# The attention stage's product order: a written table of single steps in place of a fixed rhythm

## The chip, the cores and the metric

The kernel runs on one core of one Trainium2 chip. The metric is the device time of one execution in microseconds (us). In the rows, PE is TensorE's matmuls, PEld its weight loads, DVE is VectorE, ACT is ScalarE, POOL is GpSimd and SP is SyncE. A change of under 0.3% is about what a measurement of this kernel can't tell from none.

## The reference, cut to what matters

Three layers follow each other: retention over blocks of 64 positions, a two-layer MLP with a norm ahead of it, and a causal attention of four heads (`E = 4`, called experts there) with a gate that weights each head's output per position. Only the last is touched:

```
logits = x @ w_gate;  w = softmax over the two best heads
for e in range(E):
    q, k, v = x @ wq[e], x @ wk[e], x @ wv[e]
    scores = causal(scale * (q @ k.T));  a = softmax(scores)
    ye = a @ v @ wo[e]
    out += (weight of head e, where it is among the two best) * ye
```

The shapes are 2 batches, 768 positions, model width 512, 4 heads of 64.

## The kernel before, in words

The retention and the MLP fill the first 327 us or so. Then comes the attention. TensorE's instructions stand in the order in which the code calls them (PE is scheduled by hand throughout). In the attention stage the other engines' order is made by the scheduler from the program.

The 1536 positions are four blocks of 384 (`NBLK`). For each block `qkv_steps` gives eight steps: three stretches of products for the values and the gate's logits (`value`, tile `pv`, line L786), the gate's arithmetic on DVE (`gate`, L797 to L817, with no product on PE), and four projections for queries and keys (`proj`, tile `pj`, L764). Each projection's accumulator is emptied by ACT and DVE (`qs` L771 and L772, `kh` L775, `kl` L776), and POOL copies the keys across the halves (L778). The steps of block 0 stand ahead of the loop. The 24 of blocks 1 to 3 are handed out between the attention's own steps.

The attention itself works on 12 row tiles of 128 positions, in the order `ROWS`, with 4 heads each: 48 items, numbered 0 to 47. Row tile `t` has `t + 1` tiles of 128 keys. An item goes through these steps:

- `att_s` (s): scores on PE (tile `s`, L844, one product with `kh` and one with `kl` for each 512 columns), then mask and maximum on DVE and the exponential on ACT. They lie in one of two large accumulators (`big`).
- `att_c` (c): DVE forms one over the sum and POOL scales the probabilities (`att`, L871).
- `att_t` (t): PE transposes them in 128 x 128 tiles (tile `t`, L881), and ACT copies them out to a tile `aT` (L882).
- `att_av` (v): once for each pair of heads, the products of the values with `aT` (tile `av`, L893). Two heads stand in the two 64-row halves of the output. The trace counts two records for one of these products. After a row's second pair, ACT (L899) and DVE (L900) take the result out as `avs`.
- `att_o` (o): the output product of the row from `avs` (tile `o`, L914), copied out by DVE and stored.

The accumulators of `pv`, `pj`, `t`, `av` and `o` are four buffers (`mid`) that go round.

The order was a rhythm: in turn `k` the loop calls s of item `k`, then as many of the 24 steps as a count up to `FILL = 36` asks for, c of item `k - 1`, t of item `k - 5` (`LAG`), v of the pair that ends with item `k - 7`, and o of the row that ends with item `k - 10`. A row's two stretches of v are therefore two turns apart; the last row alone has them together.

Of the kernel before, what the change touches and what calls it, by code (L numbers as in the profile page):

```python
# [8 lines left out]
F32 = mybir.dt.float32  # L9
# [8 lines left out]
P = 128  # L18
B, H, S, D = 2, 8, 768, 64
# [7 lines left out]
NBLK = B * S // TB  # L27
NTB = TB // P
# [19 lines left out]
IN_WA = ((2, 2), (3, 1), (3, 2), (0, 3), (4, 1), (5, 1))  # L48

IN_DQ = ((6, 1), (7, 1), (4, 2), (5, 2))  # L50
FILL = 36
AV_AT, O_AT = 2, 5

ROWS = ((0, 0), (0, 1), (0, 2), (0, 3), (0, 4), (1, 2), (0, 5), (1, 5), (1, 1), (1, 4), (1, 3), (1, 0))
LAG = 5
NG = FT // GF
E = 4
HD = 64
# [4 lines left out]

F64_MIN = 2.0 ** -15
F64_MAX = 122879.9921875


@with_exitstack
def model(ctx, tc, qkT, kv, lam, g_ln, w12, wat, out):
# [23 lines left out]
    def ps_mid(name):  # L93
        return psum.tile([P, 512], F32, tag="mid", bufs=4, name=name)
# [64 lines left out]
    for n, gb in enumerate(groups):  # L159
        if n == 0:  # L160
            continue
        more = []
        if n >= NBLK - 1 and n + 1 < len(groups):
            more = [("g1", *groups[n + 1], f) for f in range(GF)]
        if gb == (1, 0):
            more = [("g1", 1, 2, f) for f in range(2, GF)]
        elif gb == (1, 1):
            more = []
# [18 lines left out]
    while rest:  # L187
        for p in rest:
            ft, i = p
# [28 lines left out]
    def prep_parts(ft, i):  # L218
# [11 lines left out]
        def clamp():  # L230
            mag = t["mag"]
            nc.vector.tensor_scalar(mag, mag, F64_MAX, F64_MIN, ALU.min, ALU.max)
            nc.vector.tensor_scalar(mag.bitcast(I32), mag.bitcast(I32), 3, 0x3FFFFFFF,
# [364 lines left out]
    def mlp_step():  # L598
        n = len(steps) - len(todo)
        due = [k for k in plan if k <= n]  # L600
        if due:
            plan.pop(min(due))
        decode(1 if due else 0)
        f, args, leave = step()
        leave()
        return f, args
# [111 lines left out]
    while todo:  # L718
        f, args = mlp_step()
# [15 lines left out]
    at = ctx.enter_context(tc.tile_pool(name="at", bufs=2, side="right", reuse_waits="tile"))  # L735
# [123 lines left out]
    def att_c(b, t, e):  # L859
        row = ROW[b, t]  # L860
        n = (t + 1) * P
        pair = n <= 512
        if pair and e % 2 == 0:
            return
        for f in ((e - 1, e) if pair else (e,)):
            c = at.tile([P, 1], F32, tag="c", name=f"c{b}{t}{f}", bufs=4)
            nc.vector.tensor_scalar(c, row["ssum"][:, f:f + 1], SUM_EPS, None, ALU.add)
            nc.vector.reciprocal(c, c)  # L868
            a = row["a"][f]
            gw = GW[2 * b + t // NTB][:, t % NTB, f:f + 1]  # L870
            nc.gpsimd.tensor_scalar(a[:, :n], a[:, :n], c, gw, ALU.mult, ALU.mult)  # L871

    def att_t(b, t, e):
        row = ROW[b, t]
        a = row["a"].pop(e)
        aT = row["aT"][e] = at.tile([P, S], F32, tag="aT", name=f"aT{b}{t}{e}", bufs=6)
        for j0 in range(0, t + 1, 4):
            j1 = min(j0 + 4, t + 1)
            pt = ps_mid(f"t{b}{t}{e}{j0}")
            for j in range(j0, j1):  # L880
                nc.tensor.transpose(pt[:, (j - j0) * P:(j - j0 + 1) * P], a[:, j * P:(j + 1) * P], ident)  # L881
            nc.scalar.copy(aT[:, j0 * P:j1 * P], pt[:, :(j1 - j0) * P])  # L882

    def att_av(b, t, pr):
        row = ROW[b, t]
        v = VV[b]
        if pr == 0:
            row["pav"] = ps_one(f"av{b}{t}")
        pav = row["pav"]
        for j in range(t + 1):  # L890
            for e2 in range(2):
                e = 2 * pr + e2
                nc.tensor.matmul(pav[e2 * HD:(e2 + 1) * HD, pr * P:(pr + 1) * P], v[:, j, e * HD:(e + 1) * HD],  # L893
                                 row["aT"][e][:, j * P:(j + 1) * P], start=(j == 0), stop=(j == t),
                                 skip_group_check=True)
        if pr == 1:
            av = row["av"] = at.tile([P, 2, 2, P], F32R, tag="av", name=f"avs{b}{t}")
            pv = pav[:, :2 * P].rearrange("p (a c) -> p a c", a=2)
            nc.scalar.copy(av[:, 0], pv)  # L899
            nc.vector.tensor_tensor(av[:, 1], pv, av[:, 0].bitcast(F32), ALU.subtract)  # L900

    def att_o(b, t):
        av = ROW.pop((b, t))["av"]
        wo = WA[3].rearrange("p a (m c) -> p a m c", m=2)
        o = at.tile([P, DM], F32, tag="o", name=f"os{b}{t}")

        halves = 2 if (b, t) == ROWS[-1] else 1
        for j in range(halves):
            cs = ts(j * DM // halves, (j + 1) * DM // halves)
            po = ps_one(f"o{b}{t}{j}")  # L910
            i = 0
            for (wi, xi) in PASSES:
                for pr in range(2):
                    nc.tensor.matmul(po[:, cs], av[:, xi, pr, :], wo[:, wi, pr, cs], start=(i == 0), stop=(i == 5))  # L914
                    i += 1
            if j == 0:
                nc.vector.tensor_copy(o[:, cs], po[:, cs])
            else:
                nc.scalar.copy(o[:, cs], po[:, cs])
            (nc.sync, nc.scalar)[j].dma_start(out[b, t * P:(t + 1) * P, cs], o[:, cs])  # L920
# [2 lines left out]
        step()  # L923

    more = [step for blk in range(1, NBLK) for step in qkv_steps(blk)]
    per_blk = len(more) // (NBLK - 1)
    items = [(b, t, e) for b, t in ROWS for e in range(E)]
    done = 0
    for k in range(len(items) + LAG + O_AT + 1):
        if k < len(items):  # L930
            b, t, e = items[k]
            while done < per_blk * (2 * b + t // NTB):
                more[done]()
                done += 1
            att_s(b, t, e)
            while done < min(len(more), len(more) * (k + 1) // FILL):
                more[done]()
                done += 1
        i = k - 1
        if 0 <= i < len(items):  # L940
            att_c(*items[i])
        i = k - LAG
        if 0 <= i < len(items):
            att_t(*items[i])
        i = k - LAG - AV_AT
        if 0 <= i < len(items) and items[i][2] % 2 == 1 and i < len(items) - 1:
            b, t, e = items[i]
            att_av(b, t, e // 2)
            if i == len(items) - 3:
                att_av(b, t, 1)  # L950
        i = k - LAG - O_AT
        if 0 <= i < len(items) and items[i][2] == 3:
            att_o(*items[i][:2])


# [52 lines left out]
```

## Time and profile before

| | |
|---|---|
| median of 3 runs | 466.61 us (465.85 to 467.31) |
| the profiled execution | 466.95 us |
| its span, first to last instruction | 465.2 us |
| granted TensorE clock, mean | 1.000 |
| PE busy | 453.3 us, 97% |
| DVE, ACT, POOL busy | 334.6, 208.5, 86.6 us |

The profiled execution's time is 1.75 us longer than its span. PE's recorded end of a matmul is modelled and runs past the start of the next one, so this text takes what a product costs from start to start: the start of a row in the timeline to the start of the next row.

### The profile page before, as it was taken

The numbers are of one execution on the slowest core, as the hardware profiler recorded it, in microseconds if no ns is written. First come the engines' busy times: TensorE is split into PE (matmuls) and PEld (weight loads), VectorE is DVE, ScalarE is ACT, GpSimd is POOL, SyncE is SP. The second block draws the span as 40 slices with busy tenths as digits, with TensorE's granted clock in tenths as the row PEclk, the third lists the DMA queues.
The fourth block names the chain that finished last, engine by engine and source line by source line (L and its number), as shares of the span: only waits on it lengthen the run. The fifth ranks groups of instructions, "written<-read, shape, count | busy, mean of one in ns | idle before, by whom it ended". The sixth has DMA issues, their size and how long they took to land.

```text
span 465.2 us, 9098 instructions
## 1 busy us (share of the span) xinstructions
PE 453.3 (97%) x3562; PEld 421.0 (91%) x3563; DVE 334.6 (72%) x698; ACT 208.5 (45%) x476; POOL 86.6 (19%) x132
## 2 busy tenths in 40 slices
PE   8789999999999999999999999999999999999997
PEld 4666779999999999999999999999998898998885
DVE  5887988869778778537789745646788686586663
ACT  3568675445433213113225311311466666557673
POOL 6745500000000000000000000000055443344340
PEclk9999999999999999999999999999999999999999
DMA  7997115634421222101224412220000000001011
GB/s 281 409 359 269 48 61 190 197 90 135 138 91 50 87 92 77 60 0 47 90 92 129 155 35 51 56 65 1 0 1 0 25 25 24 23 2 38 33 45 70
DMA packets 15226, 42.33 MB, mean 91 GB/s; under 512 B 2240, under 2 KB 5072, under 8 KB 15184
## 3 DMA queue, kind: packets, MB, share of 16 engines
q1 hardware_dynamic: 14896, 41.62, 26.3%
q8 instruction: 28, 0.46, 0.4%
q10 hardware_dynamic: 288, 0.13, 0.1%
q14 instruction: 14, 0.11, 0.1%
HBM read 35.43 MB, written 6.32 MB: 90 GB/s over the span
## 4 chain that ended last, share of the span: by engine, by line
PE 73%; DVE 8%; ACT 3%; issue 1%; POOL 0%; ACTq 0%; DVEq 0%
PE y L548 27%; PE h L514 23%; PE s L844 5%; PE av L893 4%; PE t L881 4%; PE o L914 4%; PE pj L764 3%; PE pv L786 3%; DVE qs L772 1%; PE yf L570 1%; DVE kl L776 1%; DVE w L255 1%; ACT att L856 1%; DVE xn L454 0%; ACT xn L451 0%
## 5 line engine op out<-in xcount | busy, mean ns | idle before, releaser
L514 PE MATMUL h<-xn,w 128*128 128x384 f32 x768 | 139.8, 336 | 0.0
L514 PEld LDWEIGHTS h<-xn,w 128*128 128x128 f32 x768 | 133.4, 188 | 2.8 <-issue 0.8
L548 PE MATMUL y<-hs,w 128*128 128x384 f32 x552 | 99.7, 334 | 0.0
L548 PEld LDWEIGHTS y<-hs,w 128*128 128x128 f32 x552 | 96.1, 188 | 0.0
L533 ACT ACTIVATE hs<-h 128x384 fp32r<-128x384 f32 x50 | 24.5, 490 | 108.6 <-PE h L514 99.0
L778 POOL TENSOR_SCALAR kh<-kh 64x384 fp32r<-64x384 f32 x16 | 8.1, 507 | 293.1 <-ACT kh L775 291.3
L534 DVE SCALAR_TENSOR_TENSOR hs<-h,hs 128x384 fp32r<-128x384 f32 x50 | 27.7, 554 | 34.6 <-ACT hs L533 34.5
L871 POOL TENSOR_SCALAR att<-att,c,gw 128x128 f32<-128x128 f32 (+5 forms) x48 | 35.6, 747 | 51.9 <-DVE c L868 16.0
L556 DVE TENSOR_TENSOR xT<-xT,y 128x768 f32<-128x768 f32 x24 | 22.8, 951 | 28.3 <-PE y L548 28.3
L243 ACT CAST w<-top 128x512 fp32r<-128x512 f32 x32 | 19.9, 621 | 42.3 <-DVE top L237 42.3
L764 PE MATMUL pj<-x,wa 128*128 128x384 f32 x192 | 35.0, 337 | 0.0
L764 PEld LDWEIGHTS pj<-x,wa 128*128 128x128 f32 x192 | 33.3, 188 | 0.0
L882 ACT COPY aT<-t 128x512 f32<-128x512 f32 (+3 forms) x64 | 26.5, 441 | 11.2 <-PE t L881 11.0
L881 PE MATMUL t<-ident,att 128*128 128x128 f32 x168 | 26.2, 275 | 0.5 <-DVE qs L772 0.5
L252 DVE TENSOR_TENSOR top<-top,w 128x512 f32<-128x512 f32 x32 | 24.0, 750 | 0.0
L893 PE MATMUL av<-aT,v 128*64 128x128 f32 x336 | 23.7, 280 | 0.0
L844 PE MATMUL s<-kh,qs 128*128 128x512 f32 (+3 forms) x64 | 23.3, 365 | 0.0
L248 DVE SCALAR_TENSOR_TENSOR mag<-raw,mag 128x512 f32<-128x512 uint32 x31 | 22.6, 729 | 0.7
L237 DVE SCALAR_TENSOR_TENSOR top<-raw,mag 128x512 int32<-128x512 int32 x31 | 22.2, 718 | 0.5
L228 ACT ACTIVATE mag<-raw 128x512 f32<-128x512 f32 x31 | 20.5, 669 | 4.2 <-DVE w L255 2.1
L255 DVE TENSOR_TENSOR w<-top,mag 128x512 fp32r<-128x512 f32 x32 | 21.9, 684 | 0.4
L893 PEld LDWEIGHTS av<-aT,v 128*64 128x64 f32 x336 | 18.0, 136 | 4.2 <-issue 3.5
(137 smaller groups left out, 702.1 us busy)
## 6 DMA issues: line engine op xcount, KB each, us to landing
raw<-in_w SPq DMA_DIRECT2D x31, 512.0 KB, 3.7
qk<-in_qkT SPq DMA_DIRECT2D x9, 512.0 KB, 6.5
kvn<-in_kv SPq DMA_DIRECT2D x9, 512.0 KB, 6.7
xd<-xT SPq DMA_DIRECT2D x4, 768.0 KB, 4.4
xr<-xd SPq DMA_DIRECT2D x8, 384.0 KB, 3.2
out<-os SPq DMA_DIRECT2D x11, 256.0 KB, 2.0
early<-in_qkT SPq DMA_DIRECT2D x3, 512.0 KB, 8.6
early<-in_kv SPq DMA_DIRECT2D x3, 512.0 KB, 4.6
```

What stands on the lines that cost most here:

```text
L252: nc.vector.tensor_tensor(t["top"], t["top"], t["w"][:, 0].bitcast(F32), ALU.subtract)
L255: nc.vector.tensor_tensor(t["w"][:, 1], t["top"], t["mag"], ALU.add)
L514: nc.tensor.matmul(ph[:, :TB], w[:, wi, k, :], xn[:, xi, k, :], start=(i == 0), stop=(i == 11))
L533: LAST.append((nc.scalar.activation(h[:, 0], ph[:, :TB], AF.Relu), nc.vector.scalar_tensor_tensor(h[:, 1], ph[:, :TB], 0.0, h[:, 0].bitcas ...
L534: nc.vector.scalar_tensor_tensor(h[:, 1], ph[:, :TB], 0.0, h[:, 0].bitcast(F32), ALU.max, ALU.subtract)))
L548: nc.tensor.matmul(y[:, j, :TB], w[:, wi, e * P:(e + 1) * P], h[:, xi], start=(f == 0 and i == 0), stop=(f == GF - 1 and i == 2))
L764: nc.tensor.matmul(ps[:, :TB], w[:, wi, k, :], x2[:, xi, k, :], start=(i == 0), stop=(i == 11))
L844: nc.tensor.matmul(ps[:, c0:c1], q, kk[:, e, c0:c1], start=(i == 0), stop=(i == 1))
L871: nc.gpsimd.tensor_scalar(a[:, :n], a[:, :n], c, gw, ALU.mult, ALU.mult)
L881: nc.tensor.transpose(pt[:, (j - j0) * P:(j - j0 + 1) * P], a[:, j * P:(j + 1) * P], ident)
L882: nc.scalar.copy(aT[:, j0 * P:j1 * P], pt[:, :(j1 - j0) * P])
L893: nc.tensor.matmul(pav[e2 * HD:(e2 + 1) * HD, pr * P:(pr + 1) * P], v[:, j, e * HD:(e + 1) * HD], row["aT"][e][:, j * P:(j + 1) * P], star ...
```

## The change

The loop of turns goes, and with it `FILL`, `AV_AT`, `O_AT` and `LAG`. A table `ORDER` names every step in order: a letter for the step and the item's number, and `f` for the next of the 24 steps of the blocks. A row's two v stand next to each other, in 11 of the 12 rows (items 32 to 35 keep them apart). The tile `aT` has eight buffers (`AT_BUFS`) instead of six.

```diff
-FILL = 36
-AV_AT, O_AT = 2, 5
-LAG = 5
+ORDER = """
+    s0 s1 f f s2 s3 c0 s4 c1 c2 s5 c3 f s6 c4 s7 t0 t1 f c5 f t2 c6 f t3 s8 c7 s9 t4 c8 s10 v1 v3 t5 c9 c10 f t6
...
+AT_BUFS = 8
...
-        aT = row["aT"][e] = at.tile([P, S], F32, tag="aT", name=f"aT{b}{t}{e}", bufs=6)
+        aT = row["aT"][e] = at.tile([P, S], F32, tag="aT", name=f"aT{b}{t}{e}", bufs=AT_BUFS)
...
-    for k in range(len(items) + LAG + O_AT + 1):
-        if k < len(items):
-            b, t, e = items[k]
-            while done < per_blk * (2 * b + t // NTB):
-                more[done]()
-                done += 1
+    more = iter(more)
+    for op in ORDER.split():
+        if op == "f":
+            next(more)()
+            continue
+        b, t, e = items[int(op[1:])]
+        if op[0] == "s":
             att_s(b, t, e)
-            while done < min(len(more), len(more) * (k + 1) // FILL):
-                more[done]()
-                done += 1
-        i = k - 1
-        if 0 <= i < len(items):
-            att_c(*items[i])
-        i = k - LAG
-        if 0 <= i < len(items):
-            att_t(*items[i])
-        i = k - LAG - AV_AT
-        if 0 <= i < len(items) and items[i][2] % 2 == 1 and i < len(items) - 1:
...
+        elif op[0] == "v":
             att_av(b, t, e // 2)
...
```

PE has the same instructions before and after. Three places show how they moved. The line numbers of the change are 10 higher. A row's x12 counts the same instruction 12 times over.

The first place is PE at the start of the attention, where row tile (0, 0) (items 0 to 3, tile `av_3755` before) meets its values. This is before, from the transposes of item 3 to the second pair:

```order
L881 MATMUL t_3752<-ident,att_3601 128x128
L893 MATMUL av_3755<-aT_3668,v_3397 64x128
L893 MATMUL av_3755<-aT_3684,v_3397 64x128
L844 MATMUL s_3719<-kh_3395,qs_3398 128x384
L844 MATMUL s_3719<-kl_3396,qs_3398 128x384
L881 MATMUL t_3766<-ident,att_3610 128x128 x2
L844 MATMUL s_3771<-kh_3395,qs_3398 128x384
L844 MATMUL s_3771<-kl_3396,qs_3398 128x384
L764 MATMUL pj_3774<-x_1_3158,wa_2873 128x384 x12
L881 MATMUL t_3800<-ident,att_3636 128x128 x2
L893 MATMUL av_3755<-aT_3712,v_3397 64x128
L893 MATMUL av_3755<-aT_3751,v_3397 64x128
```

This is the change, where the tile is `av_3771`, from the transposes of item 4 on:

```order
L891 MATMUL t_3763<-ident,att_3602 128x128 x2
L854 MATMUL s_3768<-kh_3395,qs_3398 128x384
L854 MATMUL s_3768<-kl_3396,qs_3398 128x384
L903 MATMUL av_3771<-aT_3654,v_3397 64x128
L903 MATMUL av_3771<-aT_3658,v_3397 64x128
L903 MATMUL av_3771<-aT_3712,v_3397 64x128
L903 MATMUL av_3771<-aT_3737,v_3397 64x128
L891 MATMUL t_3780<-ident,att_3614 128x128 x2
L774 MATMUL pj_3792<-x_1_3158,wa_2873 128x384 x12
L891 MATMUL t_3810<-ident,att_3643 128x128 x2
```

The two stretches of `av` were 8 rows apart, each behind transposes. They are one now, and it stands behind scores.

The second place is PE at the output product of row tile (1, 1) (items 32 to 35; its values are `av_4921` before and `av_4948` now). This is before: the end of the next row's first stretch (`av_5023`), and then the output product `o_5049`, whose own values had ended 22 rows ahead of it:

```order
L893 MATMUL av_5023<-aT_4933,v_3545 64x128
L893 MATMUL av_5023<-aT_4965,v_3545 64x128
L844 MATMUL s_5002<-kh_3543,qs_3546 128x128
L844 MATMUL s_5002<-kl_3544,qs_3546 128x128
L881 MATMUL t_5042<-ident,att_4908 128x128 x4
L914 MATMUL o_5049<-wa_3004,avs_4979 128x512 x6
```

This is the change, from the same row's last values to its output product:

```order
L903 MATMUL av_4948<-aT_4901,v_3545 64x128
L903 MATMUL av_4948<-aT_4912,v_3545 64x128
L903 MATMUL av_4948<-aT_4901,v_3545 64x128
L903 MATMUL av_4948<-aT_4912,v_3545 64x128
L891 MATMUL t_5000<-ident,att_4892 128x128 x4
L891 MATMUL t_5006<-ident,att_4892 128x128
L854 MATMUL s_5012<-kh_3543,qs_3546 128x128
L854 MATMUL s_5012<-kl_3544,qs_3546 128x128
L924 MATMUL o_5024<-wa_3004,avs_4996 128x512 x6
```

Between a row's last values and its output product there are now four groups: the transposes of one item and one small pair of scores products.

The third place is PE at block 3's projections. This is before: the last `pv` stretch and the four projections follow each other, and then come the scores of item 28:

```order
L881 MATMUL t_4427<-ident,att_4234 128x128 x3
L786 MATMUL pv_4432<-wa_2957,x_3_3376 128x260 x12
L764 MATMUL pj_4471<-x_3_3376,wa_2873 128x384 x12
L764 MATMUL pj_4488<-x_3_3376,wa_2910 128x384 x12
L764 MATMUL pj_4509<-x_3_3376,wa_2873 128x384 x12
L764 MATMUL pj_4526<-x_3_3376,wa_2910 128x384 x12
L844 MATMUL s_4550<-kh_3543,qs_3547 128x512
L844 MATMUL s_4550<-kl_3544,qs_3547 128x512
L844 MATMUL s_4550<-kh_3543,qs_3547 128x256
L844 MATMUL s_4550<-kl_3544,qs_3547 128x256
L881 MATMUL t_4563<-ident,att_4267 128x128 x3
```

This is the change, from the block's second `pv` stretch to its second projection:

```order
L796 MATMUL pv_4365<-wa_2957,x_3_3376 128x260 x12
L796 MATMUL pv_4379<-wa_2957,x_3_3376 128x260 x12
L891 MATMUL t_4394<-ident,att_4208 128x128 x3
L854 MATMUL s_4408<-kh_3395,qs_3542 128x512
L854 MATMUL s_4408<-kl_3396,qs_3542 128x512
L854 MATMUL s_4408<-kh_3395,qs_3542 128x256
L854 MATMUL s_4408<-kl_3396,qs_3542 128x256
L891 MATMUL t_4417<-ident,att_4225 128x128 x3
L774 MATMUL pj_4451<-x_3_3376,wa_2873 128x384 x12
L891 MATMUL t_4469<-ident,att_4259 128x128 x3
L774 MATMUL pj_4474<-x_3_3376,wa_2910 128x384 x12
L903 MATMUL av_4495<-aT_4215,v_3397 64x128
```

The third `pv` stretch, two items' transposes and a scores step now stand ahead of the first projection, and a row's whole stretch of values (20 such products) stands between the second and the third.

## Rows read from the trace of the kernel before

**Rows 1.** The page: span, busy time of PE, granted clock in 40 equal slices

```profile
span 465.2 us, 9098 instructions
PE 453.3 (97%) x3562; PEld 421.0 (91%) x3563; DVE 334.6 (72%) x698; ACT 208.5 (45%) x476; POOL 86.6 (19%) x132
...
PEclk9999999999999999999999999999999999999999
```

**Rows 2.** Waits of weight loads, 320 to 466 us: total us, times, longest us

```profile
PEld av L893 <- issue: 3.5, 20, 0.3
```

**Rows 3.** PE timeline, 371 to 376 us: start us, us, instruction, count

```profile
371.67 0.62 PE L881 MATMUL t<-ident,att 128*128 128x128 f32 x4
372.05 1.65 PE L914 MATMUL o<-wa,avs 128*128 128x512 f32 x6
373.53 0.40 PE L844 MATMUL s<-kh,qs 128*128 128x512 f32 x1
...
374.17 0.62 PE L881 MATMUL t<-ident,att 128*128 128x128 f32 x4
374.72 0.88 PE L893 MATMUL av<-aT,v 128*64 128x128 f32 x12
375.53 0.50 PE L844 MATMUL s<-kh,qs 128*128 128x512 f32 x1
```

**Rows 4.** PE timeline: scores behind transposes, and transposes behind values

```profile
367.24 0.49 PE L881 MATMUL t<-ident,att 128*128 128x128 f32 x3
367.49 0.48 PE L844 MATMUL s<-kh,qs 128*128 128x512 f32 x1
...
456.71 1.09 PE L893 MATMUL av<-aT,v 128*64 128x128 f32 x16
457.74 0.44 PE L881 MATMUL t<-ident,att 128*128 128x128 f32 x2
458.11 0.94 PE L893 MATMUL av<-aT,v 128*64 128x128 f32 x8
```

**Rows 5.** The page's weight loads of `pj`, and three `pj` stretches in PE's timeline

```profile
L764 PEld LDWEIGHTS pj<-x,wa 128*128 128x128 f32 x192 | 33.3, 188 | 0.0
...
378.79 6.52 PE L764 MATMUL pj<-x,wa 128*128 128x384 f32 x36
385.14 0.34 PE L844 MATMUL s<-kh,qs 128*128 128x384 f32 x1
```

**Rows 6.** PE timeline where it stood still; in brackets idle us and who ended it

```profile
341.19 0.22 PE L844 MATMUL s<-kh,qs 128*128 128x128 f32 x1
341.55 0.33 PE L844 MATMUL s<-kl,qs 128*128 128x128 f32 x1
...
351.64 0.33 PE L844 MATMUL s<-kl,qs 128*128 128x384 f32 x1
352.49 0.41 PE L881 MATMUL t<-ident,att 128*128 128x128 f32 x2 [0.51 <-DVE qs L772]
...
417.63 1.68 PE L914 MATMUL o<-wa,avs 128*128 128x512 f32 x6 [0.24 <-DVE kl L776]
```

**Rows 7.** DVE timeline: two subtractions that those waits ended on

```profile
351.78 0.56 DVE L772 SCALAR_TENSOR_TENSOR qs<-pj,qs 64x384 fp32r<-64x384 f32 x1
...
417.02 0.56 DVE L776 TENSOR_TENSOR kl<-pj,kh 64x384 fp32r<-64x384 f32 x1
```

**Rows 8.** From a row's last values to `avs`: slowest case, then quickest (PE, DVE)

```profile
420.60 0.88 PE L893 MATMUL av<-aT,v 128*64 128x128 f32 x12
...
423.62 0.41 DVE L900 TENSOR_TENSOR avs<-av,avs 128x256 fp32r<-128x256 f32 x1
...
458.26 0.42 DVE L900 TENSOR_TENSOR avs<-av,avs 128x256 fp32r<-128x256 f32 x1 [0.86 <-ACT avs L899]
```

More of the change, by code (lines that the diff above doesn't have):

```diff
@@ L65 @@
 F64_MAX = 122879.9921875
+ORDER = """
+    s0 s1 f f s2 s3 c0 s4 c1 c2 s5 c3 f s6 c4 s7 t0 t1 f c5 f t2 c6 f t3 s8 c7 s9 t4 c8 s10 v1 v3 t5 c9 c10 f t6
+    f s11 s12 t7 s13 f t8 c11 o3 f t9 s14 t10 c12 s15 v5 c13 v7 s16 c14 f t11 s17 c15 c16 t12 c17 s18 o7 v9 v11
+    f s19 t13 f t14 f f o11 c18 f t15 s20 c19 s21 t16 s22 c20 t17 v13 v15 s23 t18 s24 f o15 s25 c21 t19 c22 c23
+    s26 t20 c24 f f t21 c25 c26 s27 t22 f c27 f t23 f v17 v19 f f s28 s29 t24 c28 o19 c29 t25 s30 v21 v23 t26
+    s31 s32 t27 o23 t28 s33 c30 t29 s34 c31 c32 s35 v25 v27 c33 c34 c35 t30 s36 c36 o27 t31 s37 c37 t32 s38 v29
+    c38 v31 t33 s39 t34 s40 t35 s41 t36 o31 c39 c40 v33 c41 s42 t37 s43 t38 v35 c42 t39 s44 c43 o35 t40 s45 c44
+    t41 s46 v37 v39 c45 t42 c46 s47 t43 v41 v43 t44 t45 o39 c47 t46 t47 v45 v47 o43 o47
+"""
+AT_BUFS = 8
 @with_exitstack
@@ L925, in model @@
     more = [step for blk in range(1, NBLK) for step in qkv_steps(blk)]
-    per_blk = len(more) // (NBLK - 1)
     items = [(b, t, e) for b, t in ROWS for e in range(E)]
-    done = 0
-    for k in range(len(items) + LAG + O_AT + 1):
-        if k < len(items):
-            b, t, e = items[k]
-            while done < per_blk * (2 * b + t // NTB):
-                more[done]()
-                done += 1
-            att_s(b, t, e)
-            while done < min(len(more), len(more) * (k + 1) // FILL):
-                more[done]()
-                done += 1
-        i = k - 1
-        if 0 <= i < len(items):
-            att_c(*items[i])
-        i = k - LAG
-        if 0 <= i < len(items):
-            att_t(*items[i])
-        i = k - LAG - AV_AT
-        if 0 <= i < len(items) and items[i][2] % 2 == 1 and i < len(items) - 1:
-            b, t, e = items[i]
-            att_av(b, t, e // 2)
[L949 to L953, printed above, removed]
+    more = iter(more)
[5 more added lines that the diff above has]
+        if op[0] == "s":
+            att_s(b, t, e)
+        elif op[0] == "c":
+            att_c(b, t, e)
+        elif op[0] == "t":
+            att_t(b, t, e)
+        elif op[0] == "v":
+            att_av(b, t, e // 2)
+        else:
+            att_o(b, t)
+    assert next(more, None) is None
 def _layouts(inp):
```

## Prediction

> **What bounds the kernel now.** I read the page first. PE is busy for 453.3 of 465.2 us, and its clock is granted in full in all 40 slices [rows 1]. Busy PE is not PE at its peak, so the next view was PE's timeline in the attention stage, read from start to start. It shows two things. PE hardly ever stands still for another engine: the timeline brackets 0.51 us once and 0.24 us once [rows 6]. But the same product takes different times, depending on what stands beside it. Four transposes take 0.38 us when an output product follows (371.67 to 372.05) and 0.55 us when a values product follows (374.17 to 374.72) [rows 3]. The recorded length of the first scores product is 0.40 us behind an output product, 0.48 us behind transposes and 0.50 us behind values [rows 3, 4]. The loads of the weights for the values sat idle 20 times without any releaser, 3.5 us in all [rows 2]. So the stage is bound by PE's own stream, and part of that stream is the price of its seams.
>
> **The price of one stretch of values.** The 12 records at 374.72 take 0.81 us to the next start, the 16 at 456.71 take 1.03 us [rows 3, 4]. The difference is 0.055 us per record, so 0.81 - 12 x 0.055 = 0.15 us is paid once per stretch. Entry from transposes adds 0.55 - 0.38 = 0.17 us. Exit into scores adds 0.50 - 0.48 = 0.02 us over scores that stand behind transposes. A stretch taken out from between transposes and scores therefore saves 0.17 + 0.15 + 0.02 = 0.34 us.
>
> **The change, part by part.** *Joining the two stretches of a row.* Before, the loop makes 24 stretches, of which the last two already touch: 23. The table joins 11 rows and leaves items 32 to 35 apart: 13. Ten stretches fewer save 10 x 0.34 = 3.4 us. The inside of a joined stretch is priced like any record, 0.055 us; the two pairs use the same tiles' shapes and the same halves.
>
> *New neighbours of the 13 that are left.* In the table seven are followed by transposes instead of scores. At 457.74 two transposes behind values and ahead of values took 0.37 us [rows 4]. Taken as two ordinary ones at 0.11 (0.55 with 0.11 or so extra for four, rows 3) and an entry of about 0.09 (the 0.17 less the 0.08 that scores pay behind transposes), 0.06 us is left for that exit, against 0.10 (0.50 - 0.40) into scores. That is 7 x 0.04 = 0.3 us less; I count 0.2, since the split is rough. Nine of the 13 are now entered from scores, output products or projections. The trace has no such entry. At the low end it costs nothing: then the 0.09 of each entry falls away and, at the most, the 0.15 per stretch too, 9 x 0.24 = 2.2 us more saved. At the high end it costs the full 0.17 that four transposes show, 9 x 0.08 = 0.7 us less saved. I take the entry from transposes as it is, the only entry that the rows show. The seams thus give 3.4 + 0.2 = 3.6 us, with bounds of 2.9 and 5.8.
>
> A rule of the Trainium skill speaks against this. Its page "TensorE: Matmul & The Clock Gate" says in "The mechanism" (packing small matmuls) that weight loads overlap with running matmuls "only when row_grp differs". All products here use all 128 rows. By that rule each load would stand by itself wherever its product is put, the order would be worth nothing, and the time would stay at 466.9. The rows speak against it: 36 `pj` products took 6.35 us from 378.79 to 385.14, 0.176 us for each with its load, while one load alone is 188 ns long [rows 5]. Loads are hidden inside a stretch.
>
> *Waits that go.* Three places. At 341.19 PE stood 0.36 us at a product of 0.22 us recorded, for the last copies of the keys; the second and third item pairs now stand behind two `pv` stretches instead of one, and 0.14 us goes. At 417.63 the output product waited 0.24 us for an accumulator that `kl` had to leave at 417.02 + 0.56 [rows 6, 7]. The third excerpt of the order shows block 3's projections spread by a scores step, transposes and a stretch of values, which is 2 us and more for DVE to catch up: 0.24 us goes. At 352.49 transposes waited 0.51 us on `qs`, which DVE began at 351.78 [rows 6, 7]. DVE's work ahead of it, block 1's gate, is the same in the change; its accumulator now goes to the first joined values (`av_3771`, first excerpt), which stand at nearly the same time. I count this wait as staying, in another place. Together 0.4 us goes.
>
> *Waits that come.* An output product needs `avs`, which ACT and DVE take out after the row's last values. The quickest case took 0.88 us from the end of the values to the end of the subtraction (456.71 + 1.09 to 458.26 + 0.42), the slowest 2.56 us (420.60 + 0.88 to 423.62 + 0.41) [rows 4, 8]. With the prices above, laid end to end along the table, the output product stands at 0.9 us behind its values for items 32 to 35 (second excerpt: five transposes and a small pair of scores products), 1.4 us for items 24 to 27, 2.4 us for items 20 to 23, and 2.5 to 8 us for the others. Queued behind it on PE are the next transposes and scores, and through them DVE, ACT and POOL. In the quickest case nothing is waited for; in the slowest, 1.7 + 1.2 + 0.2 = 3.1 us. I take values near the quick end, 0.4 and 0.1 us: 0.5 us.
>
> *The rest.* The 24 steps, the c steps and the stores issue the same instructions; no DMA is added, and none is moved past another queue. Eight `aT` buffers instead of six have no instruction. They let a row's first two transposed items wait for the joined stretch without holding up the next row's transposes. The distances from scores to transposes are 4 us or more along the table at every item, about as before. The tail, from the last values on, is in the same order as before.
>
> **The sum.** Against the profiled execution: 466.95 - 3.6 - 0.4 + 0.5 = 463.4 us. That execution is 0.3 us above the median of the runs, 466.61, so the forecast is 0.7% below the median.
>
> **The rivals.**
>
> *The waits take it back.* `avs` comes late behind other DVE work, in the mean nearer 2 us than 1. The rows show a spread of 0.88 to 2.56 us, so it is possible, but only three rows stand nearer than 2.5 us to their values. At the slowest case everywhere the sum is 463.4 - 0.5 + 3.1 = 466.0 us; half of it gives 464.5.
>
> *The entries are free and DVE is never late.* Then the seams give 5.8 us and the 0.51 goes as well: 466.95 - 5.8 - 0.9 = 460.2 us. The full sum needs all of the 0.15 to lie at the entries, while the exits must pay for some of it; half of the extra gives 461.8.
>
> *The order does nothing.* The stretches' prices are an artefact of modelled starts, or the rule on weight loads holds: 466.9 us. Against it speak the end-to-end sums: starts of later products are moved by these prices.
>
> *Slower.* The same place as the first rival, with one price: each row's output product waits until a delay D behind its values. Laid against the distances 0.9, 1.4, 2.4, 2.5, 2.9, 3.3 and more, D = 3 costs 2.1 + 1.6 + 0.6 + 0.5 + 0.1 = 4.9 us, which gives 463.4 - 0.5 + 4.9 = 467.8, and 468.0, the bound of slower, needs D a little over 3 in every row. The longest D in the trace is 2.56 us, and that once. DVE would have to be later than anywhere before, everywhere.
>
> **How the numbers follow.** The forecast as summed, 462.6 to 464.4: 0.60. Entries cheaper and waits gone, 460.4 to 462.6: 0.17. Late `avs`, 464.4 to 466.4: 0.15, of which a good third stays under 465.2. Nothing gained: 0.04. Slower: 0.04. The bound of 0.3% is 1.4 us, so faster means under 465.2: 0.60 + 0.17 + 0.06 = 0.83; same 0.13; slower 0.04. The range for 8 in 10 leaves out the far ends on both sides: 461.0 to 465.4 us.
>
> **What would show it.** In PE's timeline the groups of `av` should number 13, with joined ones of 8, 16, 24, 32, 40 and 48 records, and a joined stretch of 48 should take 48 x 0.055 + 0.15 = 2.8 us. The idle time of the loads ahead of `av` should fall from 3.5 us to about 2. The four transposes ahead of values should still take 0.55 us. A first values product behind scores should cost about what it costs behind transposes; if the scores ahead of it are no longer than elsewhere, the entry was free and the time is lower. The wait at `kl` should be gone, the one at `qs` should stand at `av`. The prediction is wrong if PE's waits in this stage add up to 3 us or more, with `avs` as releaser at the output products, or if the stage's end moves less than the stretches say.

## The result, and the profile after

The change took 462.23 us in the median of 4 runs (462.02 to 462.54), the kernel before 466.92 beside it. The ratio is 0.9904, with a 95% interval of 0.9885 to 0.9922: 1% faster, against a forecast of 463.4 us (0.7% faster) and a range of 461.0 to 465.4. The profiled execution took 462.26 us, 4.69 less than the 466.95 that the sum started from.

These are the lines of the page of the kernel after that answer to [rows 1]:

```profile
span 460.5 us, 9080 instructions
...
PE 449.3 (98%) x3562; PEld 420.5 (91%) x3563; DVE 336.5 (73%) x698; ACT 208.8 (45%) x476; POOL 86.4 (19%) x132
...
PEclk9999999999999999999999999999999999999999
```

The span is 4.7 us shorter and PE's busy time 4.0 us. PE does the same products at the same clock, so most of the gain stands in the page as less busy time for the same work. The busy share (97% before, 98% now) says nothing of it.

The waits of PE and of its weight loads from 320 to 466 us, after (what waits, line and releaser: us in total, times, longest):

```profile
PE s L854 <- POOL kl L788: 0.2, 1, 0.2
...
PEld av L903 <- issue: 1.3, 6, 0.4
```

The three waits of [rows 6] are gone, and one short one is new. The idle time of the loads ahead of the values fell from the 3.5 us of [rows 2] to 1.3; about 2 was foretold.

PE's timeline of the kernel after, at the places that the prediction speaks of (start, length as modelled, what, count, idle time ahead with its releaser):

```profile
351.02 0.42 PE L854 MATMUL s<-kh,qs 128*128 128x384 f32 x1
351.28 0.33 PE L854 MATMUL s<-kl,qs 128*128 128x384 f32 x1
...
363.49 0.39 PE L854 MATMUL s<-kl,qs 128*128 128x512 f32 x1
363.72 0.49 PE L891 MATMUL t<-ident,att 128*128 128x128 f32 x3
...
364.29 0.40 PE L854 MATMUL s<-kl,qs 128*128 128x512 f32 x1
364.61 1.09 PE L903 MATMUL av<-aT,v 128*64 128x128 f32 x16
...
367.87 0.49 PE L891 MATMUL t<-ident,att 128*128 128x128 f32 x3
368.34 0.50 PE L854 MATMUL s<-kh,qs 128*128 128x512 f32 x1
...
370.18 1.59 PE L924 MATMUL o<-wa,avs 128*128 128x512 f32 x6
371.70 1.53 PE L903 MATMUL av<-aT,v 128*64 128x128 f32 x24
...
385.77 0.71 PE L891 MATMUL t<-ident,att 128*128 128x128 f32 x5
386.24 0.42 PE L854 MATMUL s<-kh,qs 128*128 128x384 f32 x1
386.82 0.44 PE L854 MATMUL s<-kl,qs 128*128 128x384 f32 x1 [0.17 <-POOL kl L788]
387.10 0.71 PE L891 MATMUL t<-ident,att 128*128 128x128 f32 x5
387.74 1.97 PE L903 MATMUL av<-aT,v 128*64 128x128 f32 x32
...
422.91 0.82 PE L891 MATMUL t<-ident,att 128*128 128x128 f32 x6
423.48 0.37 PE L854 MATMUL s<-kh,qs 128*128 128x256 f32 x1
...
424.13 2.84 PE L903 MATMUL av<-aT,v 128*64 128x128 f32 x48
426.90 0.88 PE L891 MATMUL t<-ident,att 128*128 128x128 f32 x6
427.53 0.48 PE L854 MATMUL s<-kh,qs 128*128 128x512 f32 x1
...
443.23 1.59 PE L924 MATMUL o<-wa,avs 128*128 128x512 f32 x6
444.66 0.60 PE L891 MATMUL t<-ident,att 128*128 128x128 f32 x4
```

Five readings, all from start to start:

- *The inside of a stretch.* The 48 records at 424.13 take 2.77 us. 48 x 0.055 + 0.15 gives 2.79. The timeline has 13 groups of `av`.
- *The entry.* The same scores product takes 0.23 us ahead of transposes (363.49 to 363.72) and 0.32 us ahead of values (364.29 to 364.61). Six output products take 1.52 us ahead of values (370.18 to 371.70) and 1.43 us ahead of transposes (443.23 to 444.66). The entry costs 0.09 us from either. Five transposes take 0.47 us ahead of scores and 0.64 us ahead of values: 0.17, of which the scores behind transposes pay 0.08 in the first case, as the prediction split it. So the entry is the same from scores, output products and transposes.
- *The exit into transposes.* Six of them take 0.57 us behind scores (422.91 to 423.48) and 0.63 us behind values (426.90 to 427.53): 0.06, the value taken.
- *The new wait.* The product at 386.24 holds PE until 386.82, 0.58 us where others like it take 0.26 (351.02 to 351.28 has the same form). The trace brackets 0.17 of it.
- *A wait without a bracket.* The three transposes at 367.87 hold PE until 368.34, 0.47 us, where three ahead of scores take 0.25 (363.72 to 363.97). The weight load of those scores waited until then for an exponential on ACT (0.22 us bracketed at the load).

DVE's timeline of the kernel after, two rows, and one of ACT:

```profile
350.75 0.56 DVE L782 SCALAR_TENSOR_TENSOR qs<-pj,qs 64x384 fp32r<-64x384 f32 x1
...
442.57 0.38 ACT L909 CAST avs<-av 128x256 fp32r<-128x256 f32 x1
...
443.46 0.41 DVE L910 TENSOR_TENSOR avs<-av,avs 128x256 fp32r<-128x256 f32 x1
```

The subtraction that empties the queries' accumulator stood at 351.78 before [rows 7] and stands at 350.75 now, so the products behind it find the accumulator free. And the output product of items 32 to 35 began at 443.23, before DVE had begun the subtraction that the prediction had it wait for.

### The profile page after: what moved, and what is told of

Same layout as the page of the kernel before. It is cut to its first block, busy times and chain, and to the rows that moved or that the text cites. A ratio compares the mean times of both kernels' runs of the same rounds, so it can differ in the third digit from the quotient of the medians.

```text
span 460.5 us, 9080 instructions
## 1 busy us (share of the span) xinstructions
PE 449.3 (98%) x3562; PEld 420.5 (91%) x3563; DVE 336.5 (73%) x698; ACT 208.8 (45%) x476; POOL 86.4 (19%) x132
## 4 chain that ended last, share of the span: by engine, by line
PE 79%; DVE 4%; ACT 2%; issue 0%; POOL 0%; ACTq 0%; DVEq 0%
PE y L558 27%; PE h L524 23%; PE pj L774 7%; PE s L854 5%; PE av L903 4%; PE t L891 4%; PE pv L796 4%; PE o L924 4%; PE yf L580 1%; DVE w L265 1%; DVE xn L464 0%; ACT xn L461 0%; DVE top L247 0%; DVE top L262 0%; DVE hx L544 0%
## 5 line engine op out<-in xcount | busy, mean ns | idle before, releaser
L774 PE MATMUL pj<-x,wa 128*128 128x384 f32 x192 | 36.0, 341 | 0.0
L891 PEld LDWEIGHTS t<-ident,att 128*128 128x128 f32 x168 | 19.6, 140 | 2.9 <-issue 1.2
L903 PE MATMUL av<-aT,v 128*64 128x128 f32 x336 | 21.5, 277 | 0.0
```

The costliest lines, as they stand in the source:

```text
L774: nc.tensor.matmul(ps[:, :TB], w[:, wi, k, :], x2[:, xi, k, :], start=(i == 0), stop=(i == 11))
```

## The experiments

The theory: a price of 0.34 us per stretch of values, which is added up, and waits, which are counted one by one. The rivals: the price is not additive, or the gain comes from the spacing of steps in the table (scores ahead of exponentials above all) and the joins alone give nothing. A second question was whether the output product waits for ACT's half of `avs`, for DVE's or for both.

Each run's attention stage was worked out in the same way, from the start of its first `pv` product to the start of its last output product. "Waits" is the sum, over all rows of PE, of start to start less what that product costs between the same neighbours where nothing is late. The rest is the stretches and their neighbours. All eleven traces have the same 1046 records of products in this stage. Where nothing is late, the last product ahead of values costs the same to 0.01 us in all of them, and so does a stretch of a given length. A tenth or two of each sum is uncertain.

| kernel | stretches | time, us | ratio to before (95%) | stage against before | of it waits | rest per stretch saved |
|---|---|---|---|---|---|---|
| the change | 13 | 462.23 | 0.9904 (0.9885 to 0.9922) | -4.6 | -0.9 | 0.37 |
| e1_apart | 23 | 468.66 | 1.0036 (1.0023 to 1.0049) | +2.0 | +2.0 | |
| e2_rhythm_joined | 12 | 467.41 | 1.0006 (0.9997 to 1.0015) | +0.4 | +4.1 | 0.34 |
| e6_rhythm_joined_o4 | 12 | 465.68 | 0.9972 (0.996 to 0.9983) | -1.0 | +2.7 | 0.34 |
| e7_rhythm_joined_no_mask | 12 | 464.57 | 0.9948 (0.9932 to 0.9965) | -2.7 | +1.1 | 0.34 |
| e9_twos | 7 | 466.56 | 0.9991 (0.9979 to 1.0003) | -0.5 | +5.2 | 0.35 |
| e8_join_last | 12 | 461.80 | 0.9886 (0.9867 to 0.9905) | -5.0 | -1.0 | 0.37 |
| e3_six | 13 | 463.40 | 0.992 (0.9906 to 0.9934) | -3.6 | +0.1 | 0.37 |
| e4_o_at_once | 13 | 479.85 | 1.029 (1.0264 to 1.0316) | +12.3 | +15.7 | 0.34 |
| e5_low_first | 13 | 462.72 | 0.9915 (0.99 to 0.9929) | -3.9 | -0.2 | 0.37 |

The last column answers the first question: wherever the stretches were joined, each one less is worth 0.34 to 0.37 us, in two different orders, with 7, 12 or 13 left. What differs between the kernels is the waits.

### The table with its stretches pulled apart (e1_apart)

In ten rows the first pair's values go back to a place of their own; the rest of the table and the eight `aT` stay.

```diff
-    s0 s1 f f s2 s3 c0 s4 c1 c2 s5 c3 f s6 c4 s7 t0 t1 f c5 f t2 c6 f t3 s8 c7 s9 t4 c8 s10 v1 v3 t5 c9 c10 f t6
+    s0 s1 f f s2 s3 c0 s4 c1 c2 s5 c3 f s6 c4 s7 t0 t1 f c5 f t2 c6 f t3 v1 s8 c7 s9 t4 c8 s10 v3 t5 c9 c10 f t6
...
```

> The table of the change, but in ten of the eleven joined rows the first pair's values are moved ahead, to right behind the transposes of the row's last item (items 40 to 43: behind item 42). There are 23 stretches of values again, as before; all else stands in the change's order. Theory of the seams: ten stretches more at 0.34 to 0.36 us each, so 3.4 to 3.6 us slower than the change's 462.2, that is 465.6 to 465.8 us, with PE's waits as small as in the change. Rival, that the gain came from regrouped steps and shorter waits: within 0.7 us of the change, 462.2 to 462.9 us.

It took 468.66 us, 6.4 over the change where seams alone give 3.5. Of the stage's 6.6 us over the change, 2.9 are waits (+2.0 against -0.9 in the table) and 3.7 are the ten stretches. So the price of the stretches holds, but PE's waits did not stay as small as in the change. And the rest of the table is no better than the rhythm without the joins: with the values pulled apart it is 0.4% slower than the kernel before. The waits of PE in it, 320 to 468 us:

```profile
PE s L854 <- ACT att L858: 1.2, 2, 0.7
PE o L924 <- ACT aT L892: 0.5, 1, 0.5
```

### The rhythm with its stretches joined (e2_rhythm_joined)

The kernel before, with the values of both pairs in the turn of the second, and eight `aT`.

```diff
-        if 0 <= i < len(items) and items[i][2] % 2 == 1 and i < len(items) - 1:
+        if 0 <= i < len(items) and (items[i][2] == 3 and i < len(items) - 1 or i == len(items) - 3):
...
-            att_av(b, t, e // 2)
-            if i == len(items) - 3:
-                att_av(b, t, 1)
+            att_av(b, t, 0)
+            att_av(b, t, 1)
```

> The fixed rhythm of before, but both stretches of a row stand in the turn of the second (12 stretches instead of 23), with eight tiles of transposes. Theory of the seams: 11 x 0.34 = 3.7 us faster than before's 466.9, that is 463.2 us, and the remaining 1.0 us of the change's 4.7 us does not come. Rival, regrouping and waits: 466.2 to 466.9 us. A third case, that joined values in this rhythm hold an accumulator or the transposes up: PE waits of over 1 us with ACT as releaser, 464 us and more.

It took 467.41 us: no gain at all, against 463.2 by seams. By the time alone the rival, which saw the gain in the regrouped steps, would be right. The rows say that the stretches did save 3.7 us, and that waits took 4.1 back, most of them for exponentials on ACT. PE and then ACT at the worst place, in this kernel:

```profile
392.60 0.71 PE L881 MATMUL t<-ident,att 128*128 128x128 f32 x5
394.55 0.50 PE L844 MATMUL s<-kh,qs 128*128 128x512 f32 x1 [1.25 <-ACT att L856]
...
393.27 0.58 ACT L856 ACTIVATE att<-s,negm 128x384 f32<-128x384 f32 x1 [0.53 <-DVE negm L853]
...
393.84 0.57 ACT L856 ACTIVATE att<-s,negm 128x384 f32<-128x384 f32 x1
```

and PE at the same scores in the kernel before:

```profile
393.15 0.71 PE L881 MATMUL t<-ident,att 128*128 128x128 f32 x5
393.79 1.31 PE L893 MATMUL av<-aT,v 128*64 128x128 f32 x20
395.11 0.50 PE L844 MATMUL s<-kh,qs 128*128 128x512 f32 x1
```

There are two accumulators for scores (`big`), so a scores step waits until the exponential of the last step but one has read the same accumulator. In the kernel before, the second stretch of values (1.32 us) stood between the transposes and those scores, and covered DVE's mask and maximum and ACT's exponentials. Joined to the first, it has left the place, and PE stands. That is where the gain of a join goes in the rhythm.

### The same with quicker or later neighbours (e7_rhythm_joined_no_mask, e6_rhythm_joined_o4)

Two edits of e2 that change the spacing and no seam. The first takes DVE's causal mask out, so that future positions are not masked.

```diff
-            nc.vector.copy_predicated(ps[:, n - P:n], tri, fill)
...
```

> The rhythm with joined values, with the causal mask's operation on DVE left out, so that future positions are not masked. That takes 0.3 to 0.48 us out of the chain from scores to exponential and leaves PE's stream as it is. Theory of the two score accumulators: each of some five waits is shorter by about 0.3 us, 1.4 us in all, 466.0 us, and PE's waits for ACT's exponentials fall from 3.6 us to near 2. Rival, that the joined stretch itself is the trouble: within 0.4 us of 467.4 us.

464.57 us: 2.8 us were gained, twice what was expected. The wait above is halved, with DVE's operation gone from the chain that leads to the exponential, and the wait for `qs` at block 1's projections (0.46 us bracketed in e2) is gone as well, which was not counted (PE of this kernel):

```profile
392.98 0.50 PE L844 MATMUL s<-kh,qs 128*128 128x512 f32 x1 [0.62 <-ACT att L853]
```

The second moves the output products one turn nearer (`O_AT` 5 to 4), into the turn that the next row's first values have left.

```diff
-AV_AT, O_AT = 2, 5
+AV_AT, O_AT = 2, 4
```

> The rhythm with joined values again (467.4 us), with one number changed: each output product comes one turn earlier (O_AT 4 instead of 5). The joined stretch and the output product of a row then stand in every second turn, where the joined rhythm left three short turns in a row. Theory of the two score accumulators: scores of an item wait until the exponential of the item two before has left its accumulator, which takes 2.4 us from the end of the scores (3 to 3.5 us for pairs), and three short turns are shorter than that. Laid end to end, the joined rhythm loses 3.0 us to this in five places and this one 0.5 us in two, so 2.5 us faster than the joined rhythm: 464.9 us, between 464 and 465.5. Rival, that the joined stretch itself is the trouble (its accumulator held, the transposes' tiles, ACT's copies): no gain, 467 us and more.

465.68 us: 1.7 us gained, 2.5 expected, and 0.2 us above the range. Of PE's bracketed waits for the exponential 1.5 us are left. In both kernels the stretches stay joined and only the waits shrink, so the joined stretch itself is not the trouble: the joins' 3.7 us come back as far as the scores' spacing lets them.

### Two rows' values together (e9_twos)

The change's table with the values of two rows in one stretch, seven in all, and ten `aT`.

```diff
-... s10 v1 v3 t5 c9 c10 f t6
-    f s11 s12 t7 s13 f t8 c11 o3 f t9 s14 t10 c12 s15 v5 c13 v7 ...
+... s10 t5 c9 c10 f t6 f s11
+    s12 t7 s13 f t8 c11 f t9 s14 t10 c12 s15 v1 v3 v5 c13 v7 ...
```

> The change with the values of two rows joined in five places (7 stretches instead of 13, of up to 96 records), their two output products next to each other behind them, and ten tiles of transposes. Theory of the seams alone: 6 x 0.35 = 2.1 us faster, 460.1 us. Theory of the two score accumulators: what was between the scores is gone, and laid end to end four scores lose 3.2 us more than in the change: 463.4 us. Both hold together in what I expect, 462.5 to 464 us, with the waits at scores for ACT.

466.56 us, beside a range of 462.5 to 464 that was too good. Six stretches fewer than the change saved 2 us, and waits rose by 6:

```profile
PE s L854 <- ACT att L866: 1.7, 2, 1.1
PE s L854 <- ACT att L858: 1.5, 2, 0.8
```

The places from which values were taken lack cover again.

### The last row joined, one scores step moved (e8_join_last)

```diff
-... t16 s22 c20 t17 v13 v15 ...
+... t16 c20 t17 s22 v13 v15 ...
-... c40 v33 c41 s42 t37 s43 t38 v35 ...
+... c40 c41 s42 t37 s43 t38 v33 v35 ...
```

> The change with two moves in its table: the values of items 32 to 35 are joined as well (12 stretches instead of 13), and the scores of item 22 stand one step later, behind the transposes of item 17, where the change waited 0.32 us for POOL's copy of the keys. Theory of the seams: 0.35 us for the stretch and 0.3 us for the wait, so 461.6 us; the scores' accumulators have room in the layout. Rival, that a stretch between short steps was what kept the exponentials in time: no gain, 462.2 us or more.

461.80 us, 0.2 over the number expected. No wait of PE is bracketed in its attention stage, but only the stretch was gained. PE and its weight loads at the scores that were moved:

```profile
386.04 1.60 PE L891 MATMUL t<-ident,att 128*128 128x128 f32 x10
387.40 0.42 PE L854 MATMUL s<-kh,qs 128*128 128x384 f32 x1
...
387.31 0.14 PEld L891 LDWEIGHTS t<-ident,att 128*128 128x128 f32 x1 [0.37 <-DVE kl L786]
```

The scores of item 22 now stand behind ten transposes and find their keys. But these ten take 1.36 us, where five take 0.47 and five more at 0.11 would make it 1.0: the load of the last one waited 0.37 us for DVE's second subtraction at the same projection. So the wait has moved, from 0.32 to some 0.35 us, and the stage's 0.4 us over the change is the price of the one stretch. Against the change the two intervals overlap: it is the fastest version run here, but 0.4 us can't be told from none.

### Six transposed tiles (e3_six)

```diff
-AT_BUFS = 8
+AT_BUFS = 6
```

> The change with six tiles of transposes instead of eight. By the prediction the two more tiles let the first transposed items wait for the joined stretch. Without them ACT's copy of a later item waits until a stretch of values has been read, and the copies, exponentials and casts behind it on ACT with it. Theory: from no difference (462.2) where the stretch is over in time, to 1 us for some of the ten joined rows; I expect 463 to 465 us, with PE waiting for ACT at scores or values. Rival, that the tiles are needed for nothing: 462.0 to 462.5 us.

463.40 us, 1.2 over the change; the intervals overlap a little. At this place in it,

```profile
405.74 2.40 PE L903 MATMUL av<-aT,v 128*64 128x128 f32 x40 [0.56 <-DVE qs L782]
408.50 4.46 PE L774 MATMUL pj<-x,wa 128*128 128x384 f32 x24 [0.36 <-ACT aT L892]
...
407.96 0.86 ACT L892 COPY aT<-t 128x384 f32<-128x384 f32 x2
```

Two of ACT's copies of transposes stand at 407.96, one behind the other. In the change the same two stand at 400.93 and 403.65:

```profile
400.93 0.48 ACT L892 COPY aT<-t 128x384 f32<-128x384 f32 x1 [0.61 <-PE t L891]
...
403.65 0.47 ACT L892 COPY aT<-t 128x384 f32<-128x384 f32 x1
```

With six tiles the copies stand behind the values at 405.74, which must read theirs first, and the accumulator that the first copy should have emptied holds up the projections at 408.50. The values' own wait goes with it, as far as the rows can be read: with one of the four `mid` accumulators held, they come to stand on one that `qs` still has. "No instruction" was right of the eight tiles; they are worth some 1.0 us of waits at this place (0.63 ahead of the values and 0.42 behind them, from start to start).

### Which half the output product waits for (e4_o_at_once, e5_low_first)

In e4 each output product stands right behind its values.

```diff
-... s10 v1 v3 t5 c9 c10 f t6
-    f s11 s12 t7 s13 f t8 c11 o3 ...
+... s10 v1 v3 o3 t5 c9 c10 f
+    t6 f s11 s12 t7 s13 f t8 c11 ...
```

> The change, with each of the first eleven output products moved up to right behind its row's values. In the change the output product of items 32 to 35 began 0.23 us before DVE's subtraction for it did, so an output product needs only ACT's cast to begin, and DVE's half for the last two of its six products. Theory of the halves: each waits for the cast alone, 0.05 + 0.37 + 0.05 us less the seam's own 0.20, some 0.3 us in ten places, and for DVE's half where DVE is late by more than another 0.9 us; 3 to 5 us slower, 465 to 467 us. Theory of the prediction, that all of it is waited for (0.9 us at the quickest, in the mean nearer 1.4): 10 us and more slower, over 471 us.

479.85 us, 17.6 over the change: by the time alone on the side of the prediction's theory, whose "10 us and more" has no upper end, and far over the 3 to 5 us of the halves. The rows decide it otherwise. PE's waits of 320 to 478 us, its timeline at the first and at the worst output product, and ACT's cast at the worst:

```profile
PE o L924 <- ACT avs L909: 10.8, 12, 2.6
...
353.51 1.20 PE L924 MATMUL o<-wa,avs 128*128 128x512 f32 x4 [0.97 <-ACT avs L909]
354.99 0.74 PE L924 MATMUL o<-wa,avs 128*128 128x512 f32 x2 [0.27 <-DVE c L877]
...
378.50 1.76 PE L924 MATMUL o<-wa,avs 128*128 128x512 f32 x6 [2.59 <-ACT avs L909]
...
378.08 0.36 ACT L909 CAST avs<-av 128x256 fp32r<-128x256 f32 x1
```

The first of these shows the halves apart: four products ran when ACT's cast was done, and the last two waited again. DVE's subtraction ran there from 354.51 to 354.93, and they began at 354.99 (the name in the bracket is the operation that DVE had started next). The size is not that of the halves because ACT itself was late: at 378.08 its cast stood behind two exponentials, at 375.89 and 377.30. Neither theory had priced ACT's queue.

In e5 the change's places stay, and the order of the six products is turned, so that the first two read DVE's half.

```diff
-            for (wi, xi) in PASSES:
+            for (wi, xi) in ((0, 1), (0, 0), (1, 0)):
```

> The change with one edit: the output product's six products begin with the two that read DVE's half of `avs` (the low part) instead of ACT's half. Nothing else moves. Theory of halves: in the change the output product of items 32 to 35 began at 443.23 us on ACT's half alone (cast at 442.57 for 0.38 us), while DVE's subtraction began only at 443.46 and took 0.41. With the low half first the product can't begin before 443.46 + 0.41 = 443.87, so a wait on DVE of about 0.6 to 0.7 us must show there (the size that the prediction had counted as 0.4), and one of 0 to 0.4 us at items 24 to 27: 462.8 to 463.3 us against the change's 462.2, and DVE named as releaser of the output product. Rival theory: the output product was early in the change for another reason (DVE's half is in time by the hardware's own order, or the product waits for both halves anyway): then no wait shows and the time stays at 462.2.

DVE's and PE's rows for items 32 to 35 in it:

```profile
442.81 0.41 DVE L910 TENSOR_TENSOR avs<-av,avs 128x256 fp32r<-128x256 f32 x1
...
443.28 1.66 PE L924 MATMUL o<-wa,avs 128*128 128x512 f32 x6 [0.53 <-DVE avs L910]
```

The wait has come, at that one place and nowhere else: 0.53 us bracketed, 0.69 from start to start. The median is 462.72, 0.5 over the change and 0.1 short of the range expected; the intervals overlap, so it is the row that decides, and not the time.

## Why the prediction was right, and where its sum was not

*What bounds.* Right. PE's own stream was the bound, and its seams could be shortened.

*The price of one stretch, ten fewer.* Right. The sum had 3.4 + 0.2 = 3.6 us. Measured, the stage less its waits is 3.7 us shorter, 0.37 for each of the ten, and 0.34 to 0.37 in the eight experiments that join stretches.

*The new neighbours.* Right: 0.09 us for the entry from scores and from output products, as assumed, and 0.06 for the exit into transposes. Neither end of the bounds came.

*The rule on weight loads.* By the sentence that the prediction quotes from the Trainium skill's page "TensorE: Matmul & The Clock Gate", section "The mechanism", the order would have had no effect. This case's trace disagrees: the products were the same before and after, and their order alone, with six tiles as before (e3), was worth 0.8%.

*Waits that go.* Mis-sized: 0.4 us counted, 1.4 measured. Two reasons. The lengths in the brackets of [rows 6] were taken for the loss, and from start to start the three cost 0.30 (0.14 counted), 0.67 (0.51) and 0.48 (0.24). The last one is read with the row ahead of it, from 416.58 to 417.63, where six transposes take 0.57 elsewhere:

```profile
416.58 0.82 PE L881 MATMUL t<-ident,att 128*128 128x128 f32 x6
```

And "I count this wait as staying, in another place" failed: the wait for `qs` went. In the table the scores of the next row (items 4 to 7) come earlier. DVE's mask of their first pair stands at 345.70 in the kernel before and at 343.91 in the change, and that of the second pair at 347.06 and 345.71:

```profile
345.70 0.44 DVE L851 COPY_PREDICATED s<-tri,fill 128x256 f32<-128x256 int32 x1
...
343.91 0.42 DVE L861 COPY_PREDICATED s<-tri,fill 128x256 f32<-128x256 int32 x1
```

Before, DVE stood idle there for 0.69 and 0.58 us, and in the change for 0.34 us. DVE's work was the same, as the prediction said; its order was not. That it is the table and not the join shows in the experiments: in e2 and e6, the rhythm with joined stretches, PE still waits for `qs` there, 0.5 us bracketed, and in e1, the table with its stretches apart, it does not.

*Waits that come.* Mis-sized, and the mechanism was wrong: "an output product needs `avs`, which ACT and DVE take out" holds, for DVE's part, of its last two products alone. The first four read ACT's half, so DVE has 0.9 us longer. The 0.5 us counted did not come. Two others did, which were overlooked: 0.32 us at the keys' low half for item 22, whose scores the table puts close behind block 2's last projection, and 0.22 us ahead of the scores at 368.34, for the exponential of the last step but one. Together 0.54 us.

The sum with these sizes is 466.95 - 3.7 - 1.4 + 0.5 = 462.4 us, and the profiled execution took 462.26. The forecast was 1.1 us too high, 1.0 of it in the two terms of waits (+0.1 us together where -0.9 was measured), and inside its range.

*The distances from scores to transposes.* The one sentence, "4 us or more along the table at every item, about as before", passed over what e2 showed to decide: whether what stands between one scores step and the next but one covers the exponential. In this table it does, nearly everywhere. For e2, where it does not, the same argument forecast 463.2 us for a kernel that takes 467.4. On this point the forecast of the change was lucky: no rival of it priced this wait.

*The rivals.* Late `avs` did not take the gain back, though e4 shows that it can (2.6 us at worst, through ACT and not DVE). "The entries are free" was wrong about the entries and right that no wait for DVE's half came. That the order does nothing is out. Why the table leaves so few waits was not taken apart further: e1 and e2 show that its spacing and its joins need each other, not which single place matters most. Why an entry into values costs 0.09 us stays open too; the runs show its price alone.

## What to carry to other kernels

Where PE is busy to 97%, look at what the same product costs beside different neighbours, from start to start: seams can be added up and they hold in another order. Before moving a block of products, ask what the block covered where it stood; here the joins alone gave 3.7 us and lost 4.1 us to waits, most of them at the accumulators of the scores. For a product in several passes, the wait belongs to the operand that its first pass reads.

## What the runs showed of the hardware

Entering the products of the values, which have 64 rows of output (`128*64` in the rows), costs the product ahead of them 0.09 us, whichever of scores or output product that is (0.23 to 0.32 us, and 1.43 to 1.52 us for six). A bracketed wait understates what PE loses: 0.17 for 0.32, 0.53 for 0.69, 0.51 for 0.67, 0.24 for 0.48 us. The reason fits the rows: the modelled end of the product ahead runs past the point at which the next could have started.
